# One flag of the tile framework: the engine order is laid out against the timeline simulator instead of the default one

## The chip, the core and the metric

One core of a Trainium2 chip runs the whole program. The metric is the device time of one execution in microseconds. The kernel before has a median of 1209.55 us over 3 runs (1208.02 to 1215.54).

## The reference

Attention over 4 batches, 8 heads, 576 positions and head size 64, with a bias per head from a small network of the relative position, then two feed-forward layers over the 2304 tokens, all in float32:

```python
scores = scale * np.matmul(q, k.transpose(0, 1, 3, 2))
x = (psi_rel / psi_i)[..., None]          # log distances of positions
bias = np.maximum(x @ w1 + b1, 0.0) @ w2
scores = scores + bias.transpose(2, 0, 1)[None]
attn = softmax(scores)                    # with max subtracted
out = np.matmul(attn, v)                  # -> x of 2304 x 512
h = x @ w_in;  g = h * np.cos(h);  x = g @ w_out                                  # layer 1
h = x @ w_in;  g = np.maximum(h, 0) + alpha * np.minimum(h, 0);  x = g @ w_out    # layer 2
```

w_in is 512 x 2048 and w_out 2048 x 512 in both layers, and the weights of the layers arrive as float64.

## The kernel before, in words

**Attention.** The bias phase makes the bias of all heads in 36 groups: DVE and ACT make 128 x 576 tiles `u` (L117, L119), TensorE multiplies them by `w2` (L124), and ACT or DVE scale the result (L139, L141) and send it to DRAM as `bias_d`. Head pairs and batches give 16 pairs. Each pair is cut into 5 stages, 80 in all. A stage is one group of score matmuls (`S`, L332) into a PSUM tile of four banks that exists once, then the row minimum on DVE (L348, two of them for a full stage, one for the remainder stage), which adds the bias and frees the banks, then the exponential on ACT (L360). Between the stages a list of fillers runs on TensorE: transposes of the exponentials (L407, L416, L426), copied out of PSUM by DVE or ACT (L392, L394), and the products with v (L441, L444). The next stage's score matmuls can't start before the two instructions at L348 of the stage ahead have read the banks.

**The two layers.** Tokens are cut into 5 tiles (three of 512 and two of 384). For each layer, tile and each of 16 slices f of the hidden width there is a unit: 12 matmuls `h` (L608), the activation (layer 1: L617 to L623 on ACT and DVE with a sine on ACT at L622; layer 2: L631, L632 on DVE), a split of the result into a high part on ACT (L641) and a low part on POOL (L642), and 12 matmuls `o` (L658, L660) that add into four PSUM banks `acc`. `emit_o` of a unit follows four units behind `emit_h`. The four accumulator banks exist once. After the last unit of a tile, `evac` (L662 to L674) copies them into `oe` tiles, of which there are 3, the even ones on DVE (L670) and the odd ones on ACT (L668), and SP stores them (L672, L674). The first `o` of the next tile waits for that.

**Weights.** Each of 64 half slices is loaded, cut from its 64-bit words into float32 and split: ACT L169 and L170, DVE L172 and L173, POOL L176, ACT L184 (high part), DVE L188 (low part). `stage_w` writes some to DRAM for later (L195, fetched again at L203); `direct_w` leaves others in place. The list `bg` of such generators is advanced by a number of steps per stage or unit.

**What sets the order.** Nobody writes the order of an engine's instructions out by hand. The `TileContext` takes down the program in program order, and when its block closes a scheduler drives a simulated machine: when an engine can take another instruction, it gets the one with the best priority among those whose inputs are there in the simulated time. Priority is the place in the program, moved by `tc.high_priority(offset=...)`: 200 places for `evac`, 300 for the input splits of the next tile, 400 for all score matmuls of a stage but the first. `keep_in_program_order` ties the two weight splits (L184 and L188) behind the instruction that was taken down ahead of them on their engine. The order so found is compiled, and on the chip each engine runs its list from front to back. The simulated machine is thus the only clock that the order knows.

## Time and profile before

| what | value |
|---|---|
| runs | 1208.02, 1209.55, 1215.54 us |
| profiled execution, its own time | 1214.6 us |
| its span in the profile | 1212.8 us |
| mean granted TensorE clock of the span | 0.98 |
| TensorE busy | 1145.0 us (94%) |
| VectorE (DVE) busy | 762.1 us (63%) |
| ScalarE (ACT) busy | 536.3 us (44%) |
| GpSimd (POOL) busy | 387.1 us (32%) |

Idle time of an engine is read together with what ended it: a row such as `[5.25 <-ACT oe L668]` says that the engine had nothing running for 5.25 us and that an instruction of line 668 on ACT released it. Matmuls overlap, so 12 of them that each last 0.39 us take 2.72 us together. PEclk is the granted TensorE clock as a share of full speed.

### The profile page before, as it was taken

How to read it: one execution, taken by the hardware profiler on the slowest of the kernel's cores; microseconds unless marked ns; L12 is line 12 of the kernel's file. 1: busy time of each engine (PE TensorE's matmuls, PEld its weight loads, DVE VectorE, ACT ScalarE, POOL GpSimd, SP SyncE). 2: the span in 40 equal slices, each digit the busy share in tenths (PEclk: the TensorE clock that was granted, in tenths of full speed). 3: DMA queues.
4: the chain of work that ended last, by engine and by line, in shares of the span. 5: the costliest groups of instructions: out<-in, count | busy, mean ns of one | idle time of the engine just before them, and what ended most of it. 6: DMA issues, size and time to landing. Idle time of an engine off the chain costs nothing.

```text
span 1212.8 us, 17291 instructions
## 1 busy us (share of the span) xinstructions
PE 1145.0 (94%) x6376; PEld 900.1 (74%) x6376; DVE 762.1 (63%) x1390; ACT 536.3 (44%) x1038; POOL 387.1 (32%) x330
## 2 busy tenths in 40 slices
PE   6698998999999999799999999988999999999998
PEld 2245665666666777588888999976888888889997
DVE  8985886887668998666667667585652242242322
ACT  6875776676664664444444544443411111111111
POOL 2202332332013554233333334344542232222222
PEclk9898998999999999899999999998999999999999
DMA  7863656556136542221221325535210010010000
GB/s 229 271 176 107 216 189 204 198 174 187 70 106 198 168 132 70 70 70 61 70 70 61 105 88 183 175 123 179 70 35 35 1 52 9 9 53 1 18 9 26
DMA packets 56085, 129.48 MB, mean 107 GB/s; under 512 B 8000, under 2 KB 15168, under 8 KB 53952
## 3 DMA queue, kind: packets, MB, share of 16 engines
q1 hardware_dynamic: 53696, 111.60, 28.3%
q0 software_dynamic: 2304, 16.78, 4.3%
q8 instruction: 50, 0.82, 0.3%
q14 instruction: 35, 0.29, 0.1%
HBM read 86.53 MB, written 41.83 MB: 106 GB/s over the span
## 4 chain that ended last, share of the span: by engine, by line
PE 58%; DVE 15%; ACT 6%; issue 4%; DMA 3%; POOL 1%; DVEq 0%; ACTq 0%; SPq 0%; POOLq 0%
PE h L608 23%; PE o L660 16%; PE o L658 8%; PE S L332 3%; PE x_B L444 2%; DVE tb L620 2%; DVE tb L619 2%; DMA raw<-in_wo_dram 2%; DVE ta L618 2%; DVE wc L173 1%; ACT P L360 1%; PE x_A L444 1%; PE T_B L407 1%; ACT tb L622 1%; DVE wc L172 1%
## 5 line engine op out<-in xcount | busy, mean ns | idle before, releaser
L608 PE MATMUL h<-xhi,w 128*128 128x512 f32 (+1 forms) x1280 | 397.1, 371 | 3.3 <-DVE tb L623 3.3
L642 POOL TENSOR_TENSOR glo<-tb,ghi 128x512 fp32r<-128x512 f32 (+1 forms) x160 | 198.9, 1243 | 424.0 <-ACT ghi L641 413.5
L608 PEld LDWEIGHTS h<-xhi,w 128*128 128x128 f32 x1280 | 239.3, 189 | 38.0 <-DVE tb L623 4.2
L608 PE MATMUL h<-xlo,w 128*128 128x512 f32 (+1 forms) x640 | 237.5, 371 | 0.0
L641 ACT ACTIVATE ghi<-tb 128x512 fp32r<-128x512 f32 (+1 forms) x160 | 93.5, 584 | 296.7 <-PE o L660 259.1
L658 PE MATMUL o<-ghi,w 128*128 128x512 f32 (+1 forms) x640 | 200.5, 373 | 8.5 <-ACT oe L668 8.3
L660 PE MATMUL o<-w,ghi 128*128 128x512 f32 x576 | 193.0, 395 | 8.5 <-ACT oe L668 8.5
L631 DVE TENSOR_SCALAR tb<-h,alpha 128x512 f32<-128x512 f32 (+1 forms) x80 | 55.7, 696 | 210.5 <-PE h L608 205.9
L658 PEld LDWEIGHTS o<-ghi,w 128*128 128x128 f32 x640 | 120.2, 190 | 27.3 <-ACT oe L668 9.8
L608 PEld LDWEIGHTS h<-xlo,w 128*128 128x128 f32 x640 | 121.0, 189 | 17.4
L660 PEld LDWEIGHTS o<-w,ghi 128*128 128x128 f32 x576 | 109.1, 189 | 31.9 <-ACT oe L668 4.7
L176 POOL TENSOR_TENSOR wc<-wc,wp 128x512 int32<-128x512 int32 x64 | 87.7, 1373 | 125.2 <-DVE wc L173 107.3
L658 PE MATMUL o<-glo,w 128*128 128x512 f32 (+1 forms) x320 | 119.6, 374 | 4.4 <-POOL glo L642 4.4
L360 ACT ACTIVATE P<-P,nm 128x576 f32<-128x576 f32 x128 | 98.1, 768 | 36.8 <-DVE nm L348 36.4
L660 PE MATMUL o<-w,glo 128*128 128x512 f32 x288 | 113.6, 394 | 0.0
L622 ACT ACTIVATE tb<-tb,hpi 128x512 f32<-128x512 f32 (+1 forms) x80 | 54.3, 679 | 128.5 <-DVE tb L620 128.5
L348 DVE CUSTOM_DVE_ANT_0 P<-S,bt 128x576 f32<-128x576 f32 x128 | 91.5, 751 | 28.3 <-PE S L332 15.4
L623 DVE TENSOR_TENSOR tb<-h,tb 128x512 f32<-128x512 f32 (+1 forms) x80 | 50.8, 635 | 55.9 <-ACT tb L622 55.2
L658 PEld LDWEIGHTS o<-glo,w 128*128 128x128 f32 x320 | 60.9, 190 | 13.3 <-POOL glo L642 5.4
L332 PE MATMUL S<-kh,qh 64*128 64x288 f32 (+1 forms) x288 | 57.1, 352 | 13.8 <-DVE nm L348 13.3
L620 DVE SCALAR_TENSOR_TENSOR tb<-ta,tb 128x512 f32<-128x512 f32 (+1 forms) x80 | 68.7, 859 | 2.0
L618 DVE TENSOR_SCALAR ta<-ta 128x512 f32<-128x512 f32 (+1 forms) x80 | 47.3, 591 | 34.9 <-ACT ta L617 34.9
(98 smaller groups left out, 1628.1 us busy)
## 6 DMA issues: line engine op xcount, KB each, us to landing
raw<-in_wi_dram SPq DMA_DIRECT2D x32, 512.0 KB, 3.6
raw<-in_wo_dram SPq DMA_DIRECT2D x32, 512.0 KB, 3.8
w_d<-st SPq DMA_DIRECT2D x32, 512.0 KB, 3.1
w<-w_d POOLq DMA_DIRECT2D x16, 1024.0 KB, 7.2
bias_d<-be SPq DMA_DIRECT2D x36, 295.5 KB, 3.8
xlo<-x_d SPq DMA_DIRECT2D x24, 256.0 KB, 4.2
rq<-in_q_dram SPq DMA_DIRECT2D x16, 320.0 KB, 3.5
rk<-in_k_dram SPq DMA_DIRECT2D x16, 320.0 KB, 4.0
```

The costliest lines, as they stand in the source:

```text
L176: ge.tensor_tensor(out=c, in0=c, in1=p, op=ALU.add)
L332: te.matmul(ps[:, hf, 0:HS], lhsT=w[r, 128 * i:128 * i + 128], rhs=m[r, c0:c0 + HS], start=(j == 0), stop=(j == 2))
L348: keep(2, ve.tensor_tensor_reduce(out=sn.rearrange("p (a b) -> p a b", a=2), in0=ps[:, :, 0:HS], in1=bt[hp, s].rearrange("p (a b) -> p a b ...
L360: keep(3, se.activation(out=e, in_=e, func=AF.Exp, bias=nm, scale=-1.0, accum_out=sums[n, u][:, col:col + 1]))
L608: te.matmul(ps[:, 0:n], lhsT=w_[:, wx, w], rhs=xx[:, 0:n], start=(j == 0), stop=(j == 11))
L618: ve.tensor_scalar(tt, tt, MAGIC, MAGIC, op0=ALU.add, op1=ALU.subtract)
L620: ve.scalar_tensor_tensor(out=g, in0=tt, scalar=-C2, in1=g, op0=ALU.mult, op1=ALU.add)
L622: se.activation(out=g, in_=g, func=AF.Sin, bias=hpi)
L641: se.activation(out=ghi[:, 0:n], in_=g, func=AF.Copy)
L642: ge.tensor_tensor(out=glo[:, 0:n], in0=g, in1=ghi[:, 0:n].bitcast(F32), op=ALU.subtract)
L658: te.matmul(acc[L, t][i][:, 0:n], lhsT=w_[:, wx, wl], rhs=gx[:, 0:n], start=st, stop=sp)
L660: te.matmul(acc[L, t][i], lhsT=gx[:, sl], rhs=w_[:, wx, 512:1024], start=st, stop=sp)
```

## The change

The framework is told to schedule against its timeline simulator, in which an instruction has to get hold of the devices it uses (sequencer, engine, weight loader, DMA engines and what engines share) one after another. No instruction of the kernel, no buffer count and no priority is edited.

```diff
-    with _tile.TileContext(nc) as tc:
+    with _tile.TileContext(nc, schedule_with_timeline_sim=True) as tc:
         attn_mlp_kernel(tc, args, outs[0])
```

## Rows read from the trace of the kernel before

**Rows 1.** The page, part 1: busy us and share of the span.

```profile
PE 1145.0 (94%) x6376; PEld 900.1 (74%) x6376; DVE 762.1 (63%) x1390; ACT 536.3 (44%) x1038; POOL 387.1 (32%) x330
```

**Rows 2.** Stretches of the span: busy us (instructions), then PEclk, DMA share, GB/s.

```profile
core 0: us, PE busy (x) PEld busy (x) DVE busy (x) ACT busy (x) POOL busy (x), PEclk, DMA share, GB/s
0.00:130.00 130.00, 105.72 (x804) 50.44 (x804) 100.58 (x250) 90.40 (x187) 27.39 (x27) 0.93 0.62 192
130.00:380.00 250.00, 235.10 (x1843) 159.24 (x1840) 187.09 (x448) 164.38 (x370) 69.45 (x68) 0.98 0.52 168
380.00:490.80 110.80, 102.86 (x435) 81.84 (x433) 102.05 (x134) 64.86 (x108) 54.07 (x40) 0.98 0.42 134
490.80:506.80 16.00, 8.83 (x25) 6.69 (x25) 11.20 (x15) 7.74 (x13) 5.24 (x4) 0.79 0.40 132
812.80:830.90 18.10, 9.58 (x25) 7.29 (x25) 9.24 (x14) 7.80 (x15) 9.11 (x8) 0.72 0.76 248
830.90:1212.80 381.90, 378.01 (x1741) 321.56 (x1739) 141.57 (x208) 65.35 (x112) 112.96 (x92) 1.00 0.09 31
```

**Rows 3.** TensorE's waits over the span: us in total, times, longest us.

```profile
PE S L332 <- DVE nm L348: 13.3, 12, 2.7
PE o L660 <- ACT oe L668: 8.5, 2, 4.3
PE o L658 <- ACT oe L668: 8.3, 4, 5.3
```

**Rows 4.** Timeline of TensorE from 478 to 510 us: start, us, instruction.

```profile
482.41 0.39 PE L608 MATMUL h<-xhi,w 128*128 128x512 f32 x1
...
487.92 0.39 PE L608 MATMUL h<-xhi,w 128*128 128x512 f32 x1
...
490.42 0.39 PE L608 MATMUL h<-xhi,w 128*128 128x512 f32 x1
496.06 0.80 PE L658 MATMUL o<-ghi,w 128*128 128x512 f32 x1 [5.25 <-ACT oe L668]
...
506.84 0.39 PE L658 MATMUL o<-ghi,w 128*128 128x512 f32 x1
```

**Rows 5.** Timelines of ACT and DVE, same stretch.

```profile
492.86 1.39 DVE L188 TENSOR_TENSOR st<-wc,st 128x512 fp32r<-128x512 f32 x1 [0.35 <-ACT st L184]
...
494.28 0.66 ACT L169 ACTIVATE wc<-raw 128x512 f32<-128x512 f32 x1 [1.46 <-DVE st L188]
...
495.41 0.59 ACT L668 ACTIVATE oe<-o 128x512 f32<-128x512 f32 x1
...
496.04 0.68 DVE L670 COPY oe<-o 128x512 f32<-128x512 f32 x1
```

**Rows 6.** Timelines of TensorE, DVE and ACT from 806 to 834 us.

```profile
812.45 0.39 PE L608 MATMUL h<-xhi,w 128*128 128x512 f32 x1
817.10 0.77 PE L660 MATMUL o<-w,ghi 128*128 128x512 f32 x1 [4.26 <-ACT oe L668]
...
830.94 0.40 PE L660 MATMUL o<-w,ghi 128*128 128x512 f32 x1
...
824.45 0.49 ACT L668 ACTIVATE oe<-o 128x384 f32<-128x384 f32 x1 [6.27 <-DMA x_d<-oe]
```

**Rows 7.** The page, part 6: stores of the evacuated banks, median us to landing.

```profile
x_d<-oe SPq DMA_DIRECT2D x12, 256.0 KB, 3.3
x_d<-oe SPq DMA_DIRECT2D x8, 192.0 KB, 4.1
```

**Rows 8.** The row minimum on DVE: the page, part 5.

```profile
L348 DVE CUSTOM_DVE_ANT_0 P<-S,bt 128x576 f32<-128x576 f32 x128 | 91.5, 751 | 28.3 <-PE S L332 15.4
```

**Rows 9.** DVE lines from 380 to 500 us, busy and mean ns; then L618 over the span.

```profile
L620 DVE SCALAR_TENSOR_TENSOR tb<-ta,tb 128x512 f32<-128x512 f32 x20 | 20.7, 1036 | 0.3
L618 DVE TENSOR_SCALAR ta<-ta 128x512 f32<-128x512 f32 x20 | 16.6, 832 | 2.1 <-ACT ta L617 2.1
...
L618 DVE TENSOR_SCALAR ta<-ta x80: 344/422/1512, 381.4 to 795.5; 128x512 f32<-128x512 f32 x48, 128x384 f32<-128x384 f32 x32
```

## The prediction, made before the changed kernel was run

> **What bounds the kernel now.** I read the page's busy shares first, then the busy time by stretch, then what TensorE waits for, and last the timelines of the places where it waits. TensorE is busy for 1145.0 of 1212.8 us [rows 1], so no order can take off more than the 67.8 us in which it stands, and what the clock loses beside them. The stretches say where these are [rows 2]: 24.3 us in the first 130 us, where DVE has 100.6 us of work; 14.9 us from 130 to 380 us; 7.9 us from 380 to 490.8 us, where DVE is busy for 102.05 of 110.8 us; 7.2 us in the 16 us from 490.8 on; 8.5 us in the 18.1 us from 812.8 on. From 830.9 us to the end TensorE stands for 3.9 of 381.9 us, and from 506.8 to 812.8 us for what is left of the 67.8, 1.1 us. The last third of the kernel is TensorE's own work in program order, and an order of the engines can't shorten it.
>
> The two short stretches are the odd ones, and here the reader is to look at timelines. At 490.42 us TensorE begins the last `h` matmul that it can do, waits 5.25 us for an ACT copy of an accumulator bank, and is through with the 12 `o` matmuls and the 12 next `h` matmuls only at 506.84 [rows 4]. A unit of the same shape took 487.92 - 482.41 = 5.51 us just before [rows 4]. So 506.84 - 490.81 - 5.51 = 10.5 us are lost there, 7.2 of them standing and the rest in matmuls at 0.63 to 0.8 us, as the granted clock of the stretch is 0.79 (a part of it at 1.2 GHz after the stand, the other at 2.4) [rows 2]. The second place is the change from layer 1 to layer 2: 830.94 - 812.84 - 5.51 = 12.6 us [rows 6], with a granted clock of 0.72 [rows 2]. The two together are 23.1 us, 1.9% of the span, and by their waits they have one kind of cause: the accumulator is there once, and its copies (L668, L670) come late [rows 3].
>
> **Why they come late is a matter of order.** Ahead of the first place the last `o` of the tile is done by 487.92, since TensorE goes on to the next `h` there [rows 4]. ACT gets to the copy at 495.41 and DVE at 496.04 [rows 5]. Between stand the weight steps of the next layer: DVE L188 at 492.86 for 1.39 us, and ACT L169, which waits until L188 has let its tile go [rows 5]. `evac` has 200 places of priority over them, so a scheduler that had seen the banks ready when they are would have put the copies first. In its simulated machine DVE and ACT must have been further along than on the chip when `o` ended. The stretch ahead speaks for the same: L618 has a median of 0.422 us over the span and a mean of 0.832 us here, up to 1.512; L620 a mean of 1.036 [rows 9]. DVE is late against any model that gives an instruction one length by its shape.
>
> That length is where the skill bears on it. The Trainium skill, SBUF — State Buffer, section "Who interferes with whom", says that VectorE and GpSimd share a pair of ports as an exclusive lock, and that the order of issue decides who blocks. The spread of L618 [rows 9] agrees with it. By that rule a new order also makes new collisions, and the sum would be off by what they cost; if the lengths stayed as they are, it would not.
>
> **The change part by part.** It removes and adds no instruction and no DMA. It can move every one of the instructions, on the queues of SP and POOL too, within dependencies and buffer counts.
>
> 1. First boundary. With the copies first in line, DVE and ACT can begin near 488.4 and do two each at 0.60 to 0.68 us [rows 5], so three banks are free by 489.8, ahead of the end of `h` at 490.81. The fourth copy needs the first of three `oe` tiles back, whose store lands 3.3 us after its issue [rows 7]: 489.1 + 3.3 + 0.6 = 493.0 us. TensorE has three banks' matmuls until then, 9 x 0.23 = 2.1 us, to 492.9. Hardly a wait is left. The activation behind the copies moves back by 1.3 us, which four units of distance between `h` and `o` hide. Gain 9.5 of the 10.5 us. Bounds: 0, if nothing moves; 10.5.
> 2. Second boundary. The same, but the wait for the store is longer: ACT stood 6.27 us for it [rows 6], while the median of such stores is 4.1 us [rows 7]. With copies at about 810.8 the last bank is free at 810.8 + 4.1 to 7.4 + 0.5 = 815.4 to 818.7 us, and TensorE comes to it at 812.84 + 2.1 = 814.9. So 0.5 to 3.8 us are left of 12.6, with a fall of the clock if it is the longer. Gain 9. Bounds 0 and 12.6.
> 3. First 130 us. DVE has 100.6 us and ACT 90.4 us of work there against 105.7 on TensorE [rows 2], with long stretches in which DVE is full, so an order changes what is first and hardly the sum. Bounds: a gain of half the 24.3 us, a loss of as much. I take 0.
> 4. Attention, 130 to 380 us. TensorE stands 14.9 us in 250 and has fillers for most of DVE's time; the waits of `S` for the row minimum are 13.3 us in 12 places over the kernel [rows 2, 3]. There is more to spoil than to win: at most 15 us and the clock's 2% (5 us) can go, while one DVE instruction of 0.75 us [rows 8] put ahead of a minimum holds up the next stage. I take a loss of 3 us, bounds in the rivals.
> 5. 380 to 490.8 us. DVE's work sets the pace. TensorE stands 7.9 us; the excess of L618 over its median is 20 x 0.41 = 8.2 us [rows 9]. I take 0, bounds a gain of 8 and a loss of 20 us (third rival).
> 6. The rest: 0. TensorE is full and `h` and `o` alternate. Cover is the distance of four units between `h` and `o`; if the order used it up, each of the other seven boundaries of tiles could get a stand like the two above, 10.5 to 12.6 us.
>
> Sum: -9.5 - 9 + 3 = -15.5 us. The profiled execution took 1214.6 us for a span of 1212.8 us, 5 us over the median of the runs; 1214.6 - 15.5 = 1199.1, and by the ratio to the median 1199.1 x 1209.55 / 1214.6 = 1194.1 us. I predict 1194, 1.3% less; its own range, with one boundary won only in part and attention even or 8 us worse, is 1184 to 1205.
>
> **Rivals.**
>
> *The order is another and the time the same.* Where TensorE is full nothing shows, and the boundaries stay, because the scheduler must keep the ties of L184 and L188 behind what was taken down ahead of them and the three `oe` tiles stay three. For it: the 381.9 us from 830.9 on can hardly change [rows 2], and the fourth copy of the second place waits for a DMA. Against it: the first place waits for no DMA before 496 us. Time: 1209.5, as before.
>
> *Slower: a row minimum comes late.* Place: DVE's list in attention. If the new model sees TensorE or DVE otherwise than they run, a copy of transposes gets its place ahead of L348, and the one four-bank score tile is freed later by one DVE instruction, 0.75 us [rows 8]. There are 80 stages; at 40 of them that is 30 us; with the first boundary won (9.5) 1209.5 + 20.5 = 1230 us. It decides from 25 stages on: 25 x 0.75 = 18.8 us eats the gain of both boundaries. For it: no part of attention has slack to spare. Against it: L348 is ahead of the fillers of its own stage in program order, and the waits are now only 12.
>
> *Slower: new collisions of DVE and POOL in the first tile of layer 1.* Place: 380 to 490.8 us. If the mean of L618 and L620 there went from 0.83 and 1.04 to 1.3 and 1.5 us, 20 of each cost 20 x (0.47 + 0.46) = 19 us on the engine that sets the pace [rows 9]: 1209.5 + 19 - 9.5 = 1219 us.
>
> *Slower: new stands at other boundaries.* If the copies fall behind at two of the seven boundaries that are now free of it and the two old ones stay, it costs 2 x 11 = 22 us: 1232 us. For it: the copies depend on how far along DVE is thought to be. Against it: DVE has far more air there than at 490 us, 141.6 of 381.9 us busy [rows 2].
>
> *Much faster.* The new order also takes the stands of the first 130 us and of attention by half (12 + 7) and 2 of the 7.9 us from 380: 18.5 + 21 = 39.5 less, 1170 us. For it: many of these stands are of the same kind, an engine that holds at one instruction while another was ready. Against: full DVE.
>
> **How the numbers follow.** About 1%, 12 us, is what a measurement of this kernel can tell from no change. Forecast 0.38 (0.28 of it faster by over 1%, 0.10 within); the same time 0.15 (0.12 within, 0.02 faster, 0.01 slower); late minima 0.21 (0.17 slower, 0.04 within); collisions 0.08 (0.04 slower, 0.04 within); new stands 0.08 (slower); much faster 0.10. Together: faster 0.40, within 1% 0.30, slower 0.30. The range that holds 8 in 10 reaches from the much faster case, 1168, to a little past the late minima and the new stands, 1236; outside are both of these at their worst.
>
> **What would show it.** Right: behind the last `o` of a tile the copies L670 and L668 stand ahead of L188 and L169 on their engines, the first place loses less than 3 us and the clock is 1.00 through it; L618 to L623 keep their lengths. Wrong: TensorE waits `S <- nm` well above 13 us or attention ends after 380 us (the first rival of the slower side); the busy time of DVE from 380 us on grows (the second); or the two boundary stands are there as before, or others in place of them.

## The result, and the profile after

The changed kernel takes 1197.57 us (median of 4 runs, 1195.92 to 1199.37) against 1208.85 us for the kernel before in the same comparison: ratio 0.9891, 95% interval 0.9869 to 0.9913. The medians are 11.3 us apart (0.9%); the ratio over all the runs says 1.1% less, 0.9 to 1.3 by its interval. The profiled execution took 1197.57 us, its span is 1195.7 us; that of before was 5.7 us above its median, so the two spans differ by more (17.1 us) than the medians do.

First the same row of the page as [rows 1]. The engines run the same instructions. TensorE stands as long as before (1195.7 - 1128.2 = 67.5 us for 67.8) and is busy 16.8 us less for the same 6376 matmuls, so the busy share alone doesn't tell where the time went.

```profile
PE 1128.2 (94%) x6376; PEld 890.5 (74%) x6376; DVE 758.1 (63%) x1390; ACT 536.5 (45%) x1038; POOL 388.4 (32%) x330
```

The stretches, with the columns of [rows 2]. The last one lies where TensorE now passes from layer 1 to layer 2.

```profile
0.00:130.00 130.00, 98.07 (x790) 48.43 (x792) 102.39 (x250) 88.55 (x186) 27.32 (x27) 0.87 0.61 192
130.00:380.00 250.00, 232.46 (x1861) 154.78 (x1858) 188.45 (x445) 164.59 (x372) 69.64 (x68) 1.00 0.51 163
380.00:490.80 110.80, 102.70 (x435) 82.43 (x433) 101.54 (x137) 67.31 (x110) 57.16 (x43) 0.97 0.44 144
490.80:506.80 16.00, 11.43 (x41) 9.22 (x42) 10.65 (x17) 7.53 (x13) 4.69 (x5) 0.79 0.38 132
803.00:821.00 18.00, 18.00 (x80) 14.62 (x79) 9.45 (x14) 7.40 (x14) 6.97 (x6) 1.00 0.74 246
```

Against [rows 2] the first 130 us got worse (TensorE stands 31.9 us in place of 24.3, and its clock is 0.87 in place of 0.93), the stretch from 490.8 us got a little better at the same clock of 0.79, and the change of layers has no stand and the full clock. TensorE's waits show the same three things (the 4.9 us of `h` lie at 392.9 us, in tile 0):

```profile
PE S L332 <- DVE nm L348: 15.3, 16, 3.2
PE bps L124 <- DVE be L141: 6.9, 5, 4.0
PE h L608 <- DVE tb L623: 4.9, 1, 4.9
PE o L658 <- DVE oe L670: 4.6, 1, 4.6
```

The waits of [rows 3] for the accumulator were 16.8 us in 6 places. One of 4.6 us is left. The waits of `S` for the row minimum grew by 2 us only.

**First boundary (tile 0 to tile 1).** Timelines of DVE, ACT and TensorE, to be laid beside [rows 4, 5]:

```profile
491.95 0.68 DVE L188 TENSOR_TENSOR st<-wc,st 128x512 fp32r<-128x512 f32 x1
...
494.54 0.68 DVE L670 COPY oe<-o 128x512 f32<-128x512 f32 x1
...
492.75 0.65 ACT L169 ACTIVATE wc<-raw 128x512 f32<-128x512 f32 x1
...
493.87 0.58 ACT L668 ACTIVATE oe<-o 128x512 f32<-128x512 f32 x1
...
495.37 0.77 PE L658 MATMUL o<-ghi,w 128*128 128x512 f32 x1 [4.64 <-DVE oe L670]
...
499.35 0.63 PE L608 MATMUL h<-xlo,w 128*128 128x512 f32 x1
...
501.48 0.63 PE L658 MATMUL o<-ghi,w 128*128 128x512 f32 x2
```

The copies still come behind the weight steps L188 and L169. TensorE still stands 4.64 us. New is that `h` matmuls of the next unit (499.35) stand in its list between the `o` of banks that are free and the `o` of the bank that isn't (501.48), so the second stand of before is gone.

**Second boundary (layer 1 to layer 2).** TensorE, DVE and ACT, to be laid beside [rows 6]:

```profile
803.25 0.33 PE L658 MATMUL o<-ghi,w 128*128 128x384 f32 x1
...
806.64 0.42 PE L660 MATMUL o<-w,ghi 128*128 128x512 f32 x1
...
808.06 0.63 PE L608 MATMUL h<-xhi,w 128*128 128x512 f32 x2
...
808.75 0.40 PE L660 MATMUL o<-w,ghi 128*128 128x512 f32 x1
...
813.84 0.40 PE L660 MATMUL o<-w,ghi 128*128 128x512 f32 x1
...
805.89 0.55 DVE L670 COPY oe<-o 128x384 f32<-128x384 f32 x1
...
807.62 0.54 DVE L670 COPY oe<-o 128x384 f32<-128x384 f32 x1
...
805.13 0.47 ACT L668 ACTIVATE oe<-o 128x384 f32<-128x384 f32 x1
...
811.64 0.67 ACT L170 ACTIVATE wp<-raw 128x512 int32<-128x512 uint32 x1 [4.99 <-DMA raw<-in_wo_dram]
...
812.77 0.48 ACT L668 ACTIVATE oe<-o 128x384 f32<-128x384 f32 x1
```

The last `o` of the tile began at 803.25 us; three copies come 1.9 to 4.4 us behind it. The fourth (812.77) comes 7.6 us behind the other one on ACT, as before (7.8), but `h` matmuls fill TensorE until `o` of its bank at 813.84. It is late for another reason than before: then ACT stood 6.27 us for the store of an `oe` tile [rows 6]; now the copy shows no wait of its own, and ACT stands 4.99 us ahead of it at a weight step (L170) whose fetch has not landed.

The starts of the tiles tell best where time came and went. The table has the us between the first `h` matmuls of consecutive tiles (the 1st, 193rd, 385th ... of the span in TensorE's timeline; tiles 3 and 4 are shorter), for one profiled execution of each kernel. Executions of one order differ: by up to 3.3 us ahead of tile 0 (362.5 to 365.8 in the nine kernels below that have attention's old order), by 0.1 in tile 0 (100.5 to 100.6 in the four that share its order with before), by 1.6 in tile 1 (98.4 and 96.8 in before and copies_last), by 1.3 in tile 4 (66.9 and 68.2 in after and all_new) and by 3.0 in layer 2's tile 0 (95.1 to 98.1 in before, copies_first and copies_two).

| kernel | to tile 0 | tile 0 | tile 1 | tile 2 | tile 3 | tile 4 | layer 2, tile 0 | rest |
|---|---|---|---|---|---|---|---|---|
| before | 365.3 | 100.5 | 98.4 | 87.7 | 70.3 | 68.1 | 98.1 | 324.4 |
| after | 374.1 | 90.5 | 94.9 | 87.7 | 69.7 | 66.9 | 87.0 | 324.8 |
| all_new | 373.8 | 90.4 | 94.4 | 87.7 | 69.7 | 68.2 | 86.7 | 324.8 |
| attn_new | 378.2 | 88.2 | 101.7 | 87.7 | 70.6 | 68.1 | 96.4 | 324.4 |
| attn_old | 363.3 | 102.5 | 90.6 | 87.7 | 69.7 | 66.9 | 88.1 | 324.8 |
| pe_new | 365.7 | 101.5 | 94.2 | 87.7 | 69.7 | 68.4 | 96.3 | 324.8 |
| rest_new | 363.0 | 92.7 | 97.0 | 87.7 | 69.7 | 67.9 | 92.0 | 324.8 |
| layers_new | 362.9 | 93.2 | 94.4 | 87.7 | 69.7 | 66.9 | 85.4 | 325.3 |
| layers_copies | 365.8 | 93.3 | 88.9 | 87.7 | 69.7 | 66.9 | 85.7 | 325.2 |
| start_old | 372.5 | 84.7 | 95.5 | 87.7 | 69.7 | 66.9 | 86.3 | 324.8 |
| start_new | 367.7 | 93.3 | 95.4 | 87.7 | 69.7 | 68.2 | 87.5 | 324.8 |
| copies_first | 362.5 | 100.6 | 87.8 | 93.0 | 70.4 | 68.0 | 95.1 | 324.4 |
| copies_two | 362.6 | 100.5 | 87.9 | 87.7 | 76.5 | 68.0 | 97.1 | 324.5 |
| copies_last | 364.2 | 100.5 | 96.8 | 87.7 | 70.3 | 68.0 | 94.6 | 324.4 |

Between before and after: 8.8 us lost ahead of tile 0, 10.0 gained in it, 3.5 at the first boundary (tile 1), 1.8 in tiles 3 and 4, 11.1 at the second. The 3.5 and the 1.8 are little above the spread of one order.

### The profile page after: what moved, and what is told of

It is laid out like the page before. It is cut to its first block, busy times and chain, and to the rows that moved or that the text cites. A ratio compares the mean times of both kernels' runs of the same rounds, so it can differ in the third digit from the quotient of the medians.

```text
span 1195.7 us, 17301 instructions
## 1 busy us (share of the span) xinstructions
PE 1128.2 (94%) x6376; PEld 890.5 (74%) x6376; DVE 758.1 (63%) x1390; ACT 536.5 (45%) x1038; POOL 388.4 (32%) x330
## 4 chain that ended last, share of the span: by engine, by line
PE 53%; DVE 11%; DMA 6%; ACT 3%; issue 3%; POOL 1%; SPq 0%; DVEq 0%; ACTq 0%; POOLq 0%
PE h L608 23%; PE o L660 14%; PE o L658 10%; DMA raw<-in_wo_dram 3%; DVE tb L620 2%; PE S L332 2%; DVE wc L173 1%; DMA raw<-in_wi_dram 1%; DVE tb L619 1%; DVE w L188 1%; DVE tb L623 1%; DVE ta L618 1%; PE x_A L444 1%; PE x_B L444 1%; ACT tb L622 1%
## 5 line engine op out<-in xcount | busy, mean ns | idle before, releaser
L623 DVE TENSOR_TENSOR tb<-h,tb 128x512 f32<-128x512 f32 (+1 forms) x80 | 50.8, 635 | 62.7 <-ACT tb L622 62.3
L620 DVE SCALAR_TENSOR_TENSOR tb<-ta,tb 128x512 f32<-128x512 f32 (+1 forms) x80 | 74.8, 936 | 1.7
L170 ACT ACTIVATE wp<-raw 128x512 int32<-128x512 uint32 x64 | 42.8, 669 | 66.7 <-DMA raw<-in_wi_dram 36.5
L332 PE MATMUL S<-kh,qh 64*128 64x288 f32 (+1 forms) x288 | 56.7, 348 | 16.3 <-DVE nm L348 15.3
```

What stands on the lines that cost most here:

```text
L332: te.matmul(ps[:, hf, 0:HS], lhsT=w[r, 128 * i:128 * i + 128], rhs=m[r, c0:c0 + HS], start=(j == 0), stop=(j == 2))
L620: ve.scalar_tensor_tensor(out=g, in0=tt, scalar=-C2, in1=g, op0=ALU.mult, op1=ALU.add)
L623: ve.tensor_tensor(out=g, in0=h, in1=g, op=ALU.mult)
```

## The experiments

All but attn_old are the kernel before with an order tied on: after the last layer a list of names per engine is walked, and each instruction is made to follow the one ahead of it in its list (an edge of order alone, with no semaphore of its own). Only the lists differ. This adds three lines ahead of the kernel, so line numbers of these profiles are 3 higher (`h` is L611, the copies L671 and L673).

```diff
     attention()
     mlp()
+    import base64, json, zlib
+    at = {x.name: x for x in nc.cur_bb.bb.instructions}
+    for names in json.loads(zlib.decompress(base64.b64decode(ORDER_OF))):
+        prev = None
+        for name in (f"I-{n}" for n in names):
+            if name in at:
+                if prev is not None:
+                    tc.add_manual_dep(at[name], prev, mybir.DependencyInfo(mybir.DependencyClass.NoSync, mybir.DependencyReason.DATA), reason="order")
+                prev = name
```

**all_new: is it the order alone?** No flag, all lists of all engines from the changed kernel.

> Flag off, but every engine of the whole kernel tied to the order that the changed kernel has (up to places that the two share). If the order alone is what the flag changes: ratio 0.987 to 0.992, as the changed kernel. If the flag does something else as well (buffers, semaphores): outside of that.

1198.45 us, ratio 0.9892 (0.9874 to 0.9910). The flag does nothing but the order: in the two traces DVE and ACT run the same rows one after the other.

**attn_old and attn_new: attention against the layers, first try.** attn_old has the flag and ties only attention's instructions, to the order of before; attn_new has no flag and ties them to the order of the changed kernel.

```diff
-            if name in at:
+            if name in at and at[name][0] < n_attention:
```

> The flag stays on, but every instruction taken down in the attention function is tied, engine by engine, to the order that it has in the kernel before; the two layers are ordered by the new model. Theory A (the stretches add up: by the two traces attention lost 8.8 us to the new order and the layers gained some 20 in the median): 1188 to 1192 us, row minima at their old times (the last near 359 us), both boundaries as in the changed kernel. Rival B (the layers gain only because the new attention leaves them other work): 1203 to 1212 us. Rival C (ties of order change the layers themselves, nothing adds up): outside both.

> The mirror image: the flag is off, attention is tied to the order of the changed kernel, the layers are ordered by the old model. Theory A: 1215 to 1220 us, the first row minimum near 42 us, the boundary stands as in the kernel before. Rival B: 1195 to 1203 us.

attn_old: 1195.43 us, 0.9865 (0.9849 to 0.9881), between the cases. attn_new: 1216.47 us, 1.0040 (1.0025 to 1.0055), theory A: with attention's new order the kernel is about 5 us slower. Neither was a clean test: the layers were laid out anew in both, and their lists came out other than those meant. Of 752 instructions of the layers on DVE, 110 stand in another place in attn_old than in the changed kernel (tile 0 takes 102.5 us in the table, not 90.5), and 69 in attn_new than before. The next runs tie the layers too.

**pe_new and rest_new: TensorE's list against the others.** Attention in the old order in both; in the layers pe_new has TensorE's list of the changed kernel and the old ones elsewhere, rest_new the opposite.

> The flag is off and all orders are tied to the kernel before, but TensorE's rows of the two layers stand in the order of the changed kernel. Theory D (TensorE's list fills the wait for a bank with h matmuls of the next unit): some 11 us less from the change of layers and 2 to 3 from the first boundary, nothing from 380 to 470 us: 1195 to 1198 us. Rival E (the gain is made by ACT and DVE, whose copies and weight steps come in another order): 1206 to 1210 us.

> The other half: TensorE's list is that of the kernel before throughout, and DVE, ACT, POOL and SP have the order of the changed kernel in the rows of the two layers. Theory D: the 10 us between the end of attention and 465 us come, the boundary stands stay at two thirds or more: 1197 to 1202 us. Rival E: 1188 to 1193 us. Rival F (neither half does anything alone, only both together): 1206 to 1212 us for this and for the run with TensorE's list alone.

pe_new: 1207.17 us, 0.9957 (0.9940 to 0.9974), rival E. rest_new: 1196.15 us, 0.9874 (0.9855 to 0.9892), between D and E. Theory D, which put 11 us of the change of layers on TensorE's list, missed. Most of the layers' gain is in the lists of DVE, ACT, POOL and SP; TensorE's alone is worth 4 us. By the table tile 0 is rest_new's alone (92.7 against 101.5 us), and the change of layers needs both: 98.1 before, 96.3 with TensorE's list alone (within the spread of 95.1 to 98.1), 92.0 with the others alone, 85.4 with both (layers_new).

**layers_new: the layers' new order without attention's.** All engines' lists of the layers from the changed kernel, attention's from before.

> Flag off, attention in the order of before on all engines, the two layers in the order of the changed kernel on all engines, TensorE too. D (the parts add: rest_new's gain at the first tile and TensorE's own gain at the second boundary): 1186 to 1192 us, ratio 0.979 to 0.985. E (TensorE's order is worth nothing once the other engines have the new one): 1194 to 1198, as rest_new, ratio 0.986 to 0.989.

1189.35 us, 0.9814 (0.9792 to 0.9836): D, the parts add. Beside all_new, run with it on the same chip, attention's new order costs 1198.45 - 1189.35 = 9.1 us, and the layers' new order gives 23.0 of 1212.33 us.

**copies_first and layers_copies: term 1 by itself.** Only the copies of the first tile are moved, in the order of before and in that of layers_new. In the order of before:

```diff
 DVE: L623 tb0_1_1
+DVE: L670 oe0_0_0
 DVE: L618 ta1_2, L619 and L620 tb0_1_2
+DVE: L670 oe0_0_2
 DVE: L623 tb0_1_2, L188 st1_0_0, L172 and L173 wc1_1_0
-DVE: L670 oe0_0_0
 DVE: L618 ta1_3
-DVE: L670 oe0_0_2
 ACT: L617 ta1_2
+ACT: L668 oe0_0_1
 ACT: L622 tb0_1_2, L641 ghi0_1_1
+ACT: L668 oe0_0_3
 ACT: L184 st1_0_0, L169 wc1_1_0, L617 ta1_3
-ACT: L668 oe0_0_1
...
 SP: L590 xlo0_2_3
+SP: L672 x1_d (three stores)
 SP: L195 w_d1, L165 raw1_2_0
-SP: L672 x1_d (three stores)
```

> The kernel before with every engine tied to its old order, except at the boundary of the first tile: the two DVE copies, the two ACT copies and three of their stores stand ahead of the weight step of DVE (L188), the ACT steps L184 and L169 and the fetches of SP behind which they stood. G (term 1 of the prediction: the stand of 5.3 us there is only a matter of order and comes to the end): TensorE's wait for ACT oe and the clock's fall there go, 1198 to 1203 us against about 1209 to 1211 before, ratio 0.991 to 0.995. H (DVE, which is full there, sets the pace of the next units anyway, or the fourth copy's wait for the first store takes the place): 1206 to 1211 us, ratio over 0.996.

> layers_new and besides the four copies of the first tile and their stores moved ahead as in copies_first. G: what is left of the first boundary's 10.5 us in the changed kernel (about 7) comes to the end: 5 to 8 us less than layers_new. H: less than 3 us from layers_new.

copies_first: 1207.04 us, 0.9957 (0.9939 to 0.9976), 5.3 us less: by its ratio between G and H, by its time in H's range. layers_copies: 1184.26 us, 0.9764 (0.9743 to 0.9786), 5.1 us less than layers_new: G, and the fastest of all kernels here, 28.1 us below the 1212.33 us that before took beside it. TensorE's timeline of copies_first, at the first boundary and at the next one:

```profile
493.34 0.40 PE L611 MATMUL h<-xhi,w 128*128 128x512 f32 x1
493.57 0.40 PE L661 MATMUL o<-ghi,w 128*128 128x512 f32 x1
...
575.50 0.39 PE L611 MATMUL h<-xhi,w 128*128 128x512 f32 x1
579.63 0.76 PE L661 MATMUL o<-ghi,w 128*128 128x512 f32 x1 [3.74 <-DVE oe L673]
```

The place of 5.25 us of stand is seamless now (493.34, 493.57), and by the table tile 1 takes 87.8 us in place of 98.4: the whole 10.5 us that the prediction found there. But tile 2 takes 93.0 in place of 87.7, with a stand of 3.74 us that was not there before. A stand of TensorE is also time in which DVE and ACT catch up; without it they reach the next boundary late, and the copies with them.

**copies_two: does the lag move on?** copies_first, and the copies of the second tile moved ahead in the same way.

> copies_first, and the four copies of the second tile also moved ahead of the weight step and the split behind which they stood. L (half of copies_first's gain was given back at the second tile's boundary, where TensorE stood 3.7 us for a DVE copy, because DVE and ACT were still behind there): 4 to 6 us less than copies_first, ratio 0.990 to 0.993. M (the lag goes on to the next boundary): less than 2 us from copies_first, ratio 0.994 to 0.998.

1205.33 us, 0.9960 (0.9943 to 0.9976): M. Tile 2 is back at 87.7 us, and tile 3 takes 76.5 in place of 70.3. TensorE's timeline there:

```profile
663.22 0.41 PE L661 MATMUL o<-ghi,w 128*128 128x384 f32 x1 [2.69 <-DVE oe L673]
...
666.49 0.69 PE L661 MATMUL o<-ghi,w 128*128 128x384 f32 x1 [1.20 <-ACT oe L671]
```

So about half of what the copies give in the order of before is handed on from boundary to boundary. In layers_copies it isn't: tile 1 takes 88.9 us in place of 94.4, and tiles 2 to 4 stay as they are.

**copies_last: term 2 by itself.** The order of before, the copies of the last tile of layer 1 moved ahead in the same way.

> The kernel before with every engine tied to its old order, except at the change from layer 1 to layer 2: the two DVE copies, the two ACT copies and three of their stores stand ahead of the weight steps behind which they stood. TensorE's order is the old one. P (term 2 of the prediction: late copies alone are the 12.6 us there, and no next tile is close enough to DVE's pace to take it back): 7 to 11 us less than before, ratio 0.991 to 0.994, and the stretch from the first h of the last tile of layer 1 to that of layer 2's second 16 units (98 us before) comes to 87 to 91. Q (the fourth copy's wait for the first store is what sets the end, and only matmuls of the next unit put between, as in the changed kernel, can cover it): 0 to 4 us less, ratio 0.9965 to 1.000.

1206.68 us, 0.9956 (0.9937 to 0.9975), 4.3 us less: between P and Q. No wait for a copy is left at that place. The waits that are left come later; TensorE's from 800 to 880 us, and then the timelines of ACT and TensorE:

```profile
PE o L663 <- POOL glo L645: 4.3, 3, 2.8
```

```profile
811.19 0.47 ACT L671 ACTIVATE oe<-o 128x384 f32<-128x384 f32 x1
...
823.30 0.66 ACT L173 ACTIVATE wp<-raw 128x512 int32<-128x512 uint32 x1 [7.72 <-DMA raw<-in_wi_dram]
823.87 0.61 ACT L644 ACTIVATE ghi<-tb 128x512 fp32r<-128x512 f32 x1
...
834.28 0.50 PE L663 MATMUL o<-w,glo 128*128 128x512 f32 x1 [1.06 <-POOL glo L645]
```

The fourth copy (811.19) is no longer late. But ACT then stands 7.72 us at a weight step whose fetch has not landed, with the split L644 behind it. The weight steps of DVE and POOL come after it, POOL's part of the split (L645) stands behind POOL's weight steps, and from 834 us on `o` waits for it: 4.3 us of waits in place of the 8.5 us for bank copies there [rows 3]. That the late fetch is what delays them is read from the timelines; no run tried it.

**start_old and start_new: where attention loses 9 us.** Layers as in layers_new; attention is cut where its 28th row minimum is taken down (the expectations name the 26th, which starts at 118.5 us before, 114.0 after and 117.7 in layers_new), at some 120 us of the span on DVE and 97 us on ACT. start_old has the old lists ahead of the cut and the new ones behind it, start_new the opposite.

> Flag off, layers in the order of the changed kernel; attention in two parts: the instructions taken down up to the 26th row minimum (which before, changed and layers_new all reach at about 113 us) in the order of before, those after it in the order of the changed kernel. J (the loss of 9 us in attention is made at the start, where TensorE has done 6.5 us less by 45 us, and only shows later): about as layers_new, 1188 to 1191 us, ratio 0.980 to 0.983. K (it is made after 113 us, where the new order puts fillers of TensorE ahead of the scores): 1195 to 1199, ratio 0.986 to 0.990.

> The other way round: the first part of attention in the order of the changed kernel, the second in that of before, the layers in that of the changed kernel. J (start): 1195 to 1199 us, ratio 0.986 to 0.990. K (after 113 us): 1188 to 1191, ratio 0.980 to 0.983, although the first row minimum comes 7.6 us later.

start_old: 1187.45 us, 0.9811 (0.9787 to 0.9834). start_new: 1194.97 us, 0.9885 (0.9860 to 0.9910). J by both ratios. The first 45 us, with the columns of [rows 2], of before and then of after:

```profile
0.00:45.00 45.00, 26.83 (x233) 8.77 (x233) 38.91 (x100) 32.46 (x62) 10.54 (x12) 1.00 0.77 249
```

```profile
0.00:45.00 45.00, 26.24 (x182) 8.04 (x184) 34.97 (x78) 26.30 (x49) 13.89 (x14) 0.73 0.75 243
```

Two waits of after in the same 45 us say a part of why; below them are the rows around TensorE's longest wait there:

```profile
DVE kh L314 <- DMA rk<-in_k_dram: 3.2, 3, 1.3
...
ACT qh L312 <- DMA rq<-in_q_dram: 4.7, 3, 1.7
```

```profile
29.32 0.49 DVE L314 CAST kh<-rk 128x640 fp32r<-128x640 f32 x1 [1.34 <-DMA rk<-in_k_dram]
29.74 0.37 DVE L141 TENSOR_SCALAR be<-bps,consts,b8a 128x95 f32<-128x95 f32 x1
...
30.16 4.78 PE L124 MATMUL bps<-u,consts 128*32 128x464 f32 x24 [3.98 <-DVE be L141]
```

The new order takes casts of k and q (L314, L312) ahead of bias tiles, at places where their DMAs have not landed. DVE waits 3.2 us there (1.8 before), ACT 4.7 us (none before). Bias work stands behind them, and TensorE waits for `be`.

That is not all of it. In start_new DVE waits only 1.0 us for `rk` (1.8 in start_old), and still gets 81 instructions done in place of 101. There its bias tiles are longer. DVE's groups of the first 45 us, of start_old and then of start_new:

```profile
L122 DVE TENSOR_SCALAR u<-at,thr 128x528 f32<-128x528 f32 x4 | 1.7, 481 | 0.0
...
L122 DVE TENSOR_SCALAR u<-at,thr 128x432 f32<-128x432 f32 x4 | 1.5, 434 | 0.0
```

```profile
L122 DVE TENSOR_SCALAR u<-at,thr 128x528 f32<-128x528 f32 x4 | 4.4, 1150 | 0.0
L122 DVE TENSOR_SCALAR u<-at,thr 128x432 f32<-128x432 f32 x4 | 4.1, 1058 | 0.0
```

With the casts earlier, POOL's splits of k and q (L319, here L322) come earlier too, 8 of them in the 45 us in place of 6. Beside each of the 8 lies one bias tile that takes between 1.66 and 1.85 us, where no bias tile without POOL beside it takes over 0.52. In start_old there are 3 such tiles, in after 6. Five more at some 1.2 us each are 6 us of DVE (an estimate from these lengths).

In after DVE gets 78 instructions done in place of 100, ACT 49 in place of 62, and TensorE 182 in place of 233, and its clock falls to 0.73, a part of the time at 1.2 GHz (0.81 to 0.85 in the three other kernels that start with this order, 0.92 to 1.00 in the ten with the old one). How much of the 7.5 us between start_old and start_new is the clock, how much the waits for DMAs and how much the stretched tiles was not tried.

**What needed no run.** With 4000 places of priority for `evac` in place of 200, the scheduler gives the same order on every engine, row for row, with the flag and without. So the copies were not outbid: at their turn the simulated machine, the old one and the new one, does not see the banks ready.

## Why the prediction was right, and where it was not

The time came out as forecast: 1197.57 us for 1194, in the likeliest case's own range of 1184 to 1205, and faster by 1.1% (0.9 to 1.3, so that over 1% is likely and not certain). The breakdown did not. The forecast was 9.5 and 9 gained at the boundaries and 3 lost in attention. The profiled executions show 3.5 and 11.1 gained there, and the runs 9 lost in attention and 7 gained in tile 0, for which the forecast had 0. The last two nearly cancel, so that the sum came out this near is in part luck.

1. *First boundary, 9.5 us.* This is the step that failed, in "with the copies first in line". The size was right: copies_first shows 98.4 - 87.8 = 10.6 us to be had at the place. But the new order doesn't put them first, nor does any priority; of the row that was to show it right, L670 and L668 ahead of L188 and L169, nothing is to be seen. The 3.5 us come for the most part from TensorE's list, which doesn't wait a second time (tile 1 takes 94.2 us in pe_new and 97.0 in rest_new). The other gap in the step is that it took the gain as kept. In the order of before half of it is handed on and lost.
2. *Second boundary, 9 us.* Right in size (11.1 in these two executions; 95.1 to 98.1 us against 85.4 to 87.5 over the kernels that share each order there), right that the fourth copy stays late, though it is a weight fetch and not its store that ACT waits for ahead of it (4.99 us); but the cover is not the 3 banks' `o` matmuls that the working counted on. It is `h` matmuls between them, and three copies that come in time. Moving the copies alone gives 4.3 us (copies_last), because POOL's part of the split, behind weight steps, is the next thing late.
3. *First 130 us, 0.* Wrong: about 7.5 of the 9.1 us that attention's order costs are made here (start_new against start_old). The bounds were wide enough (half of 24.3 us either way). The words "an order changes what is first and hardly the sum" overlooked two things: an instruction taken before its DMA has landed holds up its whole engine, and an order that puts POOL's splits beside other DVE instructions changes how long those take.
4. *Attention, a loss of 3.* The part behind the cut costs nothing measurable: start_old and layers_new have ratios of 0.9811 and 0.9814. The rival of late row minima is not what happened; `S` waits 15.3 us in place of 13.3. That attention ends later (tile 0 starts at 372.5 us in start_old) is no loss by itself, since tile 0 then takes 84.7 us: more of attention was done ahead of it, and tile 1 starts at 457.2 us against 456.2.
5. *380 to 490.8 us, 0.* Wrong by 7 us, in the good direction: 100.5 to 93.2 us in layers_new, by the lists of DVE, ACT, POOL and SP (92.7 in rest_new). By the stretches of tile 0, DVE is busy 86.9 us in rest_new and 93.4 before, with 124 instructions for 127, and stands 5.8 us for 7.2; of the busy time, 2.3 us are L618, 14 times, whose mean is 690 ns for 852. So some of its work now lies behind tile 1's first `h` and some got shorter. TensorE stands 9.0 us in tile 0 before and 3.8 in rest_new: the waits for POOL's low part and for the activation go, and waits for the weight split come. Which moves do it was not tried. With the new list on DVE, ACT or SP alone, instructions wait for each other in a circle; POOL's list alone is free of that, and stays an untried candidate.
6. *The rest, 0.* Right but for 1.8 us in tiles 3 and 4, of which 1.3 can be the spread of one order; no new stand came at another boundary.

For point 5, TensorE's waits from 360 to 520 us, of before and then of rest_new:

```profile
PE o L658 <- POOL glo L642: 4.4, 3, 2.6
PE h L608 <- DVE tb L623: 3.3, 2, 1.8
```

```profile
PE h L611 <- DVE w L191: 3.6, 2, 2.1
```

The rival of new collisions between DVE and POOL did not hold at its place, though the collisions are there (where they did grow is the first 45 us, point 3). DVE's groups from 380 to 500 us, to be laid beside [rows 9]:

```profile
L620 DVE SCALAR_TENSOR_TENSOR tb<-ta,tb 128x512 f32<-128x512 f32 x20 | 25.2, 1260 | 0.2
L618 DVE TENSOR_SCALAR ta<-ta 128x512 f32<-128x512 f32 x20 | 15.2, 760 | 0.0
```

Together 40.4 us in place of 37.3, 3 us more and not 19. The Trainium skill, SBUF — State Buffer, section "Who interferes with whom", says that the order of issue decides which of the two blocks. That L620 got longer and L618 shorter under another order would fit it, but which engine issued first was not read.

## What to carry to other kernels

A stand that a timeline shows is worth its length only if the engines that were late there have slack afterwards: ask what they do while the bound engine stands, and move copies in an order in which they catch up (10.6 us at the place and 5.3 in the end, and no loss behind it in the better order). An order made by a simulated machine is as good as its times for DMAs and for instructions that another engine slows, so take it phase by phase. Here the layers of one order and the attention of the other, with four copies moved by hand, give 1184.26 us where the two orders whole give 1198.45 and 1212.33.

## What the runs showed of the hardware that was not expected

Beside POOL some of DVE's instructions stretch and others never do. Minimum, median and maximum in ns over the span of after:

```profile
L618 DVE TENSOR_SCALAR ta<-ta x80: 345/419/1528, 384.3 to 786.4; 128x512 f32<-128x512 f32 x48, 128x384 f32<-128x384 f32 x32
...
L619 DVE SCALAR_TENSOR_TENSOR tb<-ta,h x80: 536/675/690, 384.7 to 789.3; 128x512 f32<-128x512 f32 x48, 128x384 f32<-128x384 f32 x32
...
L620 DVE SCALAR_TENSOR_TENSOR tb<-ta,tb x80: 548/691/1787, 386.0 to 790.5; 128x512 f32<-128x512 f32 x48, 128x384 f32<-128x384 f32 x32
...
L623 DVE TENSOR_TENSOR tb<-h,tb x80: 538/682/693, 392.2 to 793.3; 128x512 f32<-128x512 f32 x48, 128x384 f32<-128x384 f32 x32
```

L618 and L620 read SBUF alone; L619 and L623 take `h` from PSUM. In the timelines 33 of the 80 L619 and 55 of the 80 L623 run while POOL is at work, and none is over 0.69 us. Of L618 the 49 that no POOL instruction overlaps are at most 0.43 us, the other 31 go up to 1.53. The same page of the Trainium skill says that an instruction of VectorE with at most one input in SBUF, outside the modes that use both ports, does not contend with GpSimd; L619 and L623 agree with that.
